# A chunked mLSTM cell and its feed-forward block: attention outputs cross DRAM by feature groups, four tokens side by side, on one queue

## The chip, the cores and the metric

The kernel runs on one core of a Trainium2 chip. TensorE multiplies matrices into PSUM, VectorE, ScalarE and GpSimd work element by element, and SyncE (SP) issues most of the DMA transfers. The metric is the device time in microseconds; lower is better.

## The reference

The inputs are q, k, v and an output gate, each of 4 batches x 8 heads x 768 tokens x 40 features in float32, and two gates per head and token. The first half is a recurrence over tokens with a stabilised running maximum `m`; the second half is a two-layer feed-forward block on the outputs.

```python
for t in range(S):
    m_new = np.maximum(f_gate[:, :, t] + m, i_gate[:, :, t])
    f_stab, i_stab = np.exp(f_gate[:, :, t] + m - m_new), np.exp(i_gate[:, :, t] - m_new)
    C = f_stab * C + i_stab * outer(v_t, k_t)          # per batch and head
    n, m = f_stab * n + i_stab * k_t, m_new
    y[:, :, t] = sigmoid(o_t) * (C @ q_t) / np.maximum(np.abs(n @ q_t), 1.0)
x = y.transpose(0, 2, 1, 3).reshape(B * S, H * D)      # 3072 tokens x 320 features
h = x @ w_in                                           # 320 x 2048
out = (h * sigmoid(1.702 * h)) @ w_out                 # 2048 x 320
```

## The kernel before, in words

**Windows.** The 768 tokens are cut into six windows `w` of 128 tokens. Inside a window the recurrence is written as masked products (`scores`, `values`); from window to window a state is carried (`scale`, `carry`, `decay`). Each window has 4 batches; from w = 1 on, attention works on two pairs of batches, `c` = 0 and 1. The feed-forward block then takes the 4 x 128 = 512 tokens of the window at once: `up_fast` (first layer with GELU, tokens as columns) and `down_fast` (second layer, tokens as rows); for w = 0 these are `up` and `down`.

**Order of work.** Instructions of each engine run in the order in which the program is written; there is no scheduler. While `down_fast(w)` gives TensorE 14 blocks of products (for w = 0 `down` gives 16), the attention of window w + 1 is put between them: `attention` (L786) holds a list of steps and, in `at`, the block after which each stands. For w + 1 > 1 these are: `columns`, the two `scale` and the two `decay` after block 0, `carry` after 3, `scores` after 4, `values` and `seam_in` of c = 0 after 5 and of c = 1 after 6, `seam_turn` of c = 0 after 10 and of c = 1 after 12. For w + 1 = 1 they are spread over 16 blocks, `seam_turn` after 13 and 14.

**Outputs and the turn.** `outputs` (L410) ends with two VectorE instructions (L424), one for each batch of the pair; each writes 128 tokens (partitions) x 320 features of the tile `y`. The feed-forward block needs features on partitions and tokens as columns, `xT`. For w = 0 TensorE transposes (`seam`). For w > 0 `y` goes through a DRAM tile: `x_row<-y` writes both batches in one transfer (L431), and `seam_in` (L489) brings them back in eight loads of 32 rows each, four of 64 and four of 32 features wide (L495), into a free part of `q_sq`, so that `seam_turn` (L497) can finish with VectorE's transposition of 32 x 32 blocks (L499). For c = 0 the write and all loads are on SP's queue; for c = 1 the write and four loads are on ScalarE's, four loads on SP's.

**Stores.** `down_fast` (L705) makes two output tiles `o` per `c` from a pool of two buffers. `product` (L715) adds a PSUM result to a part of `o` on VectorE (L721, L723); `store` (L725) sends one batch's 128 x 320 rows to `out` (L727): store(1) after block 5 or 12, store(0) after 6 or 13. The first products of c = 1 write into the buffers that the stores of c = 0 read. PSUM results come from a pool of four buffers.

**Semaphores of transfers.** Each transfer is given one of eight semaphores in turn, over both queues, and its instruction waits until the transfer that had that semaphore before has landed. A waiting instruction holds up all that stands behind it on its queue.

**GpSimd.** For each window it runs two `scale` (L514, `vw` from v), two `decay` (L507, `state_mid`), then the masks of `weights` (L385). `scale` needs ScalarE's L329, `decay` its L333, which comes after it. `carry` (L516) multiplies `k` with `vw` on TensorE (L524) and adds to `state_mid` on VectorE (L533).

Of the kernel before, what the change touches and what calls it, by code (L numbers as in the profile page):

```python
# [8 lines left out]
FP = mybir.dt.float32  # L9
# [8 lines left out]
L = 128  # L18
# [8 lines left out]
def kernel(  # L27
# [12 lines left out]
    nc = tc.nc  # L40
    B, H, S, D = q.shape
    BH = B * H
    DM = H * D
# [21 lines left out]
    rows = ctx.enter_context(tc.tile_pool(name="rows", bufs=2, space=bass.MemoryType.DRAM))  # L65
# [154 lines left out]
    kT, qT, ys, xT, gs, o_ps, sums, vw, x_row = {}, {}, {}, {}, {}, {}, {}, {}, {}  # L220
# [189 lines left out]
    def outputs(w, hs, u):  # L410

        n = hs.stop - hs.start
        c, b = divmod(hs.start // H, 2)
        den = work.tile([L, n, 1], FP, tag="den", name="den")
        V.tensor_scalar(out=den, in0=u[:, :, D:D1], scalar1=-1.0, scalar2=1.0, op0=OP.mult, op1=OP.max)
        V.tensor_tensor(out=den, in0=u[:, :, D:D1], in1=den, op=OP.max)
        V.reciprocal(out=den, in_=den)
        z = eo[w][:, hs, :]
        V.scalar_tensor_tensor(out=z, in0=z, scalar=1.0, in1=u[:, :, 0:D], op0=OP.add, op1=OP.mult)  # L419
        if b == 0:  # L420
            ys[w, c] = work.tile([L, 2, DM + 64], FP, tag="y", name="y")
        for x in range(n // H):
            y, h = ys[w, c][:, b + x], slice(hs.start + x * H, hs.start + x * H + H)
            V.scalar_tensor_tensor(out=y[:, 0:DM].rearrange("p (h d) -> p h d", d=D), in0=eo[w][:, h, :], scalar=0.5,  # L424
                                   in1=den[:, x * H:(x + 1) * H].to_broadcast([L, H, D]), op0=OP.mult, op1=OP.mult)
        y = ys[w, c][:, b:b + n // H]
        if w == 0:
            G.tensor_copy(out=y[:, :, DM:DM + 64], in_=y[:, :, DM - 64:DM])
            return
        x = x_row[w, c] = rows.tile([2 * L, DM], FP, name="x_row")  # L430
        (nc.scalar if c else nc.sync).dma_start(out=x.rearrange("(b t) d -> t b d", b=2), in_=y[:, :, 0:DM])  # L431

    def values(w, c):
        if w == 0:
            hs = slice(c * H, (c + 1) * H)
            po = ps_m.tile([L, H, D1], FP, tag="m", name="p_o")
            for p in range(NP):
                for i in range(2):
                    h = 2 * p + i
                    T.matmul(po[:, h, :], wt[w, c][:, p, i, :], v_st[:, c * H + h, :], start=True, stop=True)  # L440
            outputs(w, hs, po)
            return
# [21 lines left out]
        V.tensor_tensor(out=v, in0=view(pi), in1=g.to_broadcast([L, 2, NJ, D1]), op=OP.mult)  # L464
        V.tensor_tensor(out=v, in0=view(po), in1=v, op=OP.add)  # L465
        outputs(w, hs, u)

    def x_of(w):
# [15 lines left out]
    def x_square(c, n):  # L484

        at, m = (c * 768, 64) if n == 0 else (c * 768 + 512, 32)
        return q_sq[:, at:at + 8 * m].rearrange("r (b y) -> r b y", y=m)

    def seam_in(w, c):  # L489
        x = x_row[w, c].rearrange("(b r) d -> r b d", r=32)  # L490
        for n, m in ((0, 64), (1, 32)):
            for g in range(4):
                at = g * 64 if n == 0 else 256 + g % 2 * 32
                queue = nc.scalar if c and g % 2 else nc.sync
                queue.dma_start(out=x_square(c, n)[g * 32:g * 32 + 32], in_=x[:, :, at:at + m])  # L495

    def seam_turn(w, c):  # L497
        for n, k in ((0, slice(0, 2)), (1, slice(2, 3))):
# [200 lines left out]
    def last_sums(w, c, js):  # L699

        for j in js:
            s2 = sums[w, 2, j // 2][:, j % 2, :, c]
            V.tensor_tensor(out=s2, in0=hidden(w, j + 4, 0)[:, :, c], in1=s2, op=OP.subtract)

    def down_fast(w, c):  # L705
        o = [op.tile([128, DM], FP, tag="o", name="o_sb") for _ in range(2)]
        o00, o01, o10, o11 = (o[i][:, n * DH:(n + 1) * DH] for i in range(2) for n in range(2))

        def block(two, k):
            return lambda f: gs[w, k * 4 + f // 2][:, f % 2, (2 * c + two) * L:(2 * c + two + 1) * L]  # L710

        def total(x):
            return lambda f: sums[w, x, f // 4][:, f // 2 % 2, f % 2, c, :]

        def product(a, b, *adds):  # L715
            po = ps_m.tile([128, DH], FP, tag="m", name="p_out")
            for f in range(NH):
                T.matmul(po, a(f), b[:, f, :], start=(f == 0), stop=(f == NH - 1))  # L718
            for dst, x in adds:
                if x is None:  # L720
                    V.tensor_copy(out=dst, in_=po)  # L721
                else:
                    V.tensor_tensor(out=dst, in0=x, in1=po, op=OP.add)  # L723

        def store(two):  # L725
            b = 2 * c + two
            nc.sync.dma_start(out=out[b * S + w * L:b * S + (w + 1) * L, :], in_=o[two])  # L727

        return [lambda: product(block(0, 0), w00, (o11, None)),
                lambda: product(block(0, 1), w10, (o00, o11)),  # L730
                lambda: (product(total(2), t2, (o01, o11)), last_sums(w, c, (0, 1))),
                lambda: product(block(1, 0), w01, (o10, o01)),
                lambda: (last_sums(w, c, (2, 3)), product(total(1), t1, (o11, o10), (o01, o01))),
                lambda: (product(block(1, 1), t4, (o10, o10)), store(1)),
                lambda: (product(total(2), w11, (o01, o01)), store(0))]


# [47 lines left out]

    def attention(w):  # L786
        at = (0, 1, 3, 3, 5, 6, 8, 9, 13, 14) if w == 1 else (0, 0, 1, 3, 1, 4, 5, 6, 10, 12)
        calls = [[(columns, w), (scale, w, 0), (scale, w, 1), (decay, w, 0, 0), (decay, w, 1, 0)],
                 [(weights, w, 0)], [(weights, w, 1)], [(carry, w, 0), (carry, w, 1)], [(open_gates, w)],
                 [(scores, w, 0), (scores, w, 1)], [(values, w, 0), (seam_in, w, 0)], [(values, w, 1), (seam_in, w, 1)],  # L790
                 [(seam_turn, w, 0)], [(seam_turn, w, 1)]]
        side = {}
        for i, c in zip(at, calls):
            side.setdefault(i, []).extend(c)
        return side

    for w in range(NW):
# [19 lines left out]
        else:  # L817
# [20 lines left out]
            gelu_fast(w, NF // 2 - 1)  # L838
            run([(hidden_sums, w, j, late) for late in (False, True) for j in (2, 3)])
        side = attention(w + 1) if more else {}  # L840
        if w == 0:
            columns_turn(1)
# [47 lines left out]
```

## Time and profile before

| | |
|---|---|
| time, median of 3 runs | 489.41 us (488.73 to 489.68) |
| time of the profiled execution | 493.03 us |
| its span, first to last instruction | 491.3 us |
| mean granted TensorE clock | 0.997 |
| write `x_row<-y`, issue to landing (median) | 2.3 us on SP, 2.7 us on ScalarE's queue |
| loads `q_sq<-x_row`, 64 KB, issue to landing (median) | 2.2 us on SP, 2.4 us on ScalarE's queue |
| stores `out_dram<-o_sb`, 160 KB, issue to landing (median) | 1.9 us |
| issue of one load `q_sq<-x_row` on SP (median) | 0.45 us |

The profile is of one execution, which took somewhat longer than the runs without a profile. Times in its views count from the first instruction. A wait is put down to the instruction or transfer that ended it last; L-numbers are lines of the kernel before. PE is TensorE, PEld its weight loads, DVE VectorE, ACT ScalarE, POOL GpSimd, and SPq and ACTq are the queues of SyncE and ScalarE. "xT", "x_row", "o_sb" and the like are tiles by the program's names.

### The profile page before, as it was taken

The page shows a single profiled execution, that of the slowest core. Times are in us where ns is not written, and L with a number is a line of the kernel's source. Part 1 is how long each engine was busy: PE and PEld are TensorE (multiplying, and loading weights), DVE is VectorE, ACT ScalarE, POOL GpSimd, SP SyncE. Part 2 cuts the span into 40 slices and gives each one's busy share as a digit, 9 for nine tenths or more (in the row PEclk, how much of TensorE's full clock was granted, in tenths as well). Part 3 has the DMA queues.
Part 4 walks back from the last instruction along what each step waited for, and adds up shares of the span by engine and source line. Part 5 has one row for each costly group of instructions (what it writes and reads, how often), then busy time and mean ns, then how long its engine had stood idle before and what let it go on. Part 6 is the DMA issues. An engine that isn't in the chain of part 4 may idle for free. (4 is left out here: it accounts for less than half of the span.)

```text
span 491.3 us, 12085 instructions
## 1 busy us (share of the span) xinstructions
PE 475.3 (97%) x4926; PEld 380.6 (77%) x4926; DVE 348.1 (71%) x691; ACT 189.8 (39%) x429; POOL 148.8 (30%) x135
## 2 busy tenths in 40 slices
PE   8999999999999999999999999999999999999997
PEld 5774446776678889767889867899877899776997
DVE  5675976987788974868974968984968963653822
ACT  3745559700354800444900254810254810064200
POOL 6020004300397800127610137720136720035300
PEclk9999999999999999999999999999999999899999
DMA  8999987004998214999204899104799304100000
GB/s 182 175 313 142 261 124 197 3 29 119 205 153 121 27 44 104 168 165 131 42 29 121 149 179 141 38 17 128 142 163 136 67 17 111 50 2 0 1 27 29
DMA packets 160472, 52.20 MB, mean 106 GB/s; under 512 B 132736, under 2 KB 157856, under 8 KB 160416
## 3 DMA queue, kind: packets, MB, share of 16 engines
q1 hardware_dynamic: 153616, 48.80, 53.9%
q10 hardware_dynamic: 6800, 2.62, 1.9%
q8 instruction: 39, 0.64, 0.6%
q14 instruction: 17, 0.14, 0.1%
HBM read 43.86 MB, written 7.54 MB: 105 GB/s over the span
## 5 line engine op out<-in xcount | busy, mean ns | idle before, releaser
L658 POOL TENSOR_TENSOR g<-g,parts 128x512 f32<-128x512 f32 x30 | 38.3, 1276 | 221.2 <-DVE parts L650 210.1
L646 ACT COPY parts<-p_h 128x256 f32<-128x256 f32 x40 | 15.0, 374 | 168.1 <-DMA out_dram<-o_sb 84.8
L718 PE MATMUL p_out<-w_out_sb,g 128*128 128x160 f32 x480 | 71.0, 302 | 3.7 <-DVE g L694 3.5
L718 PEld LDWEIGHTS p_out<-w_out_sb,g 128*128 128x128 f32 x480 | 66.8, 190 | 5.9 <-DVE g L694 4.5
L616 PE MATMUL p_h<-xT,w_in_sb 128*128 128x256 f32 x240 | 67.0, 388 | 0.8 <-DVE xT L499 0.8
L597 ACT ACTIVATE g<-g 128x512 f32<-128x512 f32 x80 | 50.0, 631 | 36.0 <-DVE g L653 24.8
L616 PEld LDWEIGHTS p_h<-xT,w_in_sb 128*128 128x128 f32 x240 | 43.6, 190 | 21.3 <-issue 7.6
L723 DVE TENSOR_TENSOR o_sb<-o_sb,p_out 128x160 f32<-128x160 f32 x70 | 20.4, 316 | 48.8 <-DMA out_dram<-o_sb 28.3
L718 PE MATMUL p_out<-t_sb,s 128*128 128x160 f32 x320 | 47.1, 300 | 0.0
L718 PEld LDWEIGHTS p_out<-t_sb,s 128*128 128x128 f32 x320 | 44.4, 190 | 0.2
L649 DVE TENSOR_TENSOR t_x<-p_h,parts 128x256 f32<-128x256 f32 x40 | 16.7, 417 | 39.2 <-PE p_h L621 34.7
L616 PE MATMUL p_h<-t_x,s_in 128*128 128x256 f32 x160 | 41.1, 379 | 0.7 <-DVE t_x L586 0.7
L621 PE MATMUL p_h<-xT,w_in_x 64*128 64x512 f32 x160 | 39.7, 615 | 0.0
L381 ACT ACTIVATE wt<-wt,cols 128x64 f32<-128x64 f32 x160 | 38.8, 335 | 0.1
L667 PE MATMUL p_out<-w_out_sb,g 128*128 128x320 f32 x128 | 36.0, 436 | 0.7 <-DVE w_out_sb L234 0.7
L514 POOL TENSOR_TENSOR vw<-v_st,cols 128x656 f32<-128x656 f32 x12 | 18.9, 1593 | 57.3 <-ACT cols L329 57.3
L616 PEld LDWEIGHTS p_h<-t_x,s_in 128*128 128x128 f32 x160 | 30.3, 190 | 5.2 <-issue 1.1
L667 PEld LDWEIGHTS p_out<-w_out_sb,g 128*128 128x128 f32 x128 | 23.8, 190 | 10.6 <-DVE w_out_sb L234 1.2
L650 DVE TENSOR_TENSOR parts<-p_h,t_x 128x512 f32<-128x512 f32 x40 | 27.7, 692 | 3.5
L546 PE MATMUL p_h<-xT,w_in_sb 128*128 128x512 f32 x64 | 29.5, 604 | 0.1
L657 ACT COPY g<-p_h 128x512 f32<-128x512 f32 x30 | 17.4, 581 | 31.4 <-PE p_h L621 26.1
L653 DVE TENSOR_TENSOR g<-p_h,parts 128x512 f32<-128x512 f32 x40 | 27.7, 691 | 1.4
(185 smaller groups left out, 845.8 us busy)
## 6 DMA issues: line engine op xcount, KB each, us to landing
wt<-m_row SPq DMA_DIRECT2D x40, 128.0 KB, 3.8
k_sq<-in_k_dram SPq DMA_DIRECT2D x16, 320.0 KB, 6.3
q_sq<-in_q_dram SPq DMA_DIRECT2D x16, 320.0 KB, 10.3
out_dram<-o_sb SPq DMA_DIRECT2D x24, 160.0 KB, 1.9
eo<-in_o_gate_dram SPq DMA_DIRECT2D x5, 640.0 KB, 9.5
bits<-in_moe_w_in_dram SPq DMA_DIRECT2D x6, 512.0 KB, 6.9
v_st<-in_v_dram SPq DMA_DIRECT2D x14, 160.0 KB, 4.7
bits<-in_moe_w_out_dram SPq DMA_DIRECT2D x6, 320.0 KB, 5.5
```

What stands on the lines that cost most here:

```text
L381: A.activation(out=x[:, h, :], in_=x[:, h, :], func=AF.Exp, scale=-1.0, bias=cols[w][:, c * PH + h:c * PH + h + 1])
L514: G.tensor_tensor(out=vw[w, c], in0=v_st[:, hs, :], in1=e, op=OP.mult)
L546: T.matmul(ph[j][i], w_in_sb[:, c, f * 128:(f + 1) * 128], x[:, c, :], start=(first and c == 0), stop=(not first and c == 1))
L597: A.activation(out=gs[w, j][:, i, :], in_=gs[w, j][:, i, :], func=AF.Gelu_apprx_sigmoid)
L616: T.matmul(out, a, x[n], start=start, stop=stop)
L621: T.matmul(row, w_in_x[r, j, :], rest_x[r, 2, :], start=not late, stop=late)
L650: V.tensor_tensor(out=y[:, half_w:3 * half_w].rearrange("p (a t) -> p a t", a=2), in0=flat[:, half_w:3 * half_w].rearrange("p (a t) -> p a ...
L653: V.tensor_tensor(out=g[:, 1, :], in0=row1, in1=y[:, half_w:3 * half_w], op=OP.add)
L658: G.tensor_tensor(out=g0, in0=g0, in1=u, op=OP.add)
L667: T.matmul(po, gs[w, f // 2][:, f % 2, b * L:(b + 1) * L], w_out_sb[:, f, :], start=(f == 0), stop=(f == NF - 1))
L718: T.matmul(po, a(f), b[:, f, :], start=(f == 0), stop=(f == NH - 1))
L723: V.tensor_tensor(out=dst, in0=x, in1=po, op=OP.add)
```

## The change

`seam_out` replaces the one write per pair: after each of the two L424 instructions two transfers go out, one for features 0 to 255 as four groups of 64 and one for features 256 to 319 as two groups of 32, into two DRAM tiles laid out by group, then token, then feature. In such a group four consecutive tokens lie side by side, so `seam_in` reads lines of 4 x 64 floats (1 KB) or 4 x 32 floats (512 B): one load of 128 partitions and two of 64 (the 32-wide part is needed on two halves of the partitions). That is four writes and three loads for each `c`, all on SP's queue. Partition r of a block of 32 now holds tokens 4r to 4r + 3 where it held tokens r, 32 + r and so on; the columns of `xT` therefore stand in the order 32 n + r for token 4 r + n, all products keep that order, and `store` of `down_fast` writes rows to DRAM with a step of four: an access of 4 x 32 x 320 in place of 128 x 320. The stores of `down` (w = 0) stay as they are. Apart from this, the list in `attention` puts the two `decay` ahead of the two `scale`.

```diff
--- before.py
+++ after.py
@@ -423,12 +423,11 @@
             y, h = ys[w, c][:, b + x], slice(hs.start + x * H, hs.start + x * H + H)
             V.scalar_tensor_tensor(out=y[:, 0:DM].rearrange("p (h d) -> p h d", d=D), in0=eo[w][:, h, :], scalar=0.5,
                                    in1=den[:, x * H:(x + 1) * H].to_broadcast([L, H, D]), op0=OP.mult, op1=OP.mult)
-        y = ys[w, c][:, b:b + n // H]
-        if w == 0:
+            if w:
+                seam_out(w, c, x)
+        if w == 0:
+            y = ys[w, c][:, b:b + n // H]
             G.tensor_copy(out=y[:, :, DM:DM + 64], in_=y[:, :, DM - 64:DM])
-            return
-        x = x_row[w, c] = rows.tile([2 * L, DM], FP, name="x_row")
-        (nc.scalar if c else nc.sync).dma_start(out=x.rearrange("(b t) d -> t b d", b=2), in_=y[:, :, 0:DM])
 
     def values(w, c):
         if w == 0:
@@ -486,13 +485,23 @@
         at, m = (c * 768, 64) if n == 0 else (c * 768 + 512, 32)
         return q_sq[:, at:at + 8 * m].rearrange("r (b y) -> r b y", y=m)
 
+    def seam_out(w, c, b):
+
+        if b == 0:
+            x_row[w, c] = (rows.tile([2, 4, L, 64], FP, name="x_row"), rows.tile([2, 2, L, 32], FP, name="x_rest"))
+        y = ys[w, c][:, b, :]
+        for x, at, m in ((x_row[w, c][0], 0, 64), (x_row[w, c][1], 256, 32)):
+            g = x.shape[1]
+            nc.sync.dma_start(out=x[b].rearrange("g t y -> t g y"),
+                              in_=y[:, at:at + g * m].rearrange("t (g y) -> t g y", y=m))
+
     def seam_in(w, c):
-        x = x_row[w, c].rearrange("(b r) d -> r b d", r=32)
-        for n, m in ((0, 64), (1, 32)):
-            for g in range(4):
-                at = g * 64 if n == 0 else 256 + g % 2 * 32
-                queue = nc.scalar if c and g % 2 else nc.sync
-                queue.dma_start(out=x_square(c, n)[g * 32:g * 32 + 32], in_=x[:, :, at:at + m])
+        for n, gs_ in ((0, (0,)), (1, (0, 64))):
+            x = x_row[w, c][n]
+            g, y = x.shape[1], x.shape[3]
+            for r in gs_:
+                nc.sync.dma_start(out=x_square(c, n)[r:r + g * 32].rearrange("p (b n) y -> p b (n y)", b=2),
+                                  in_=x.rearrange("b g (r n) y -> (g r) b (n y)", n=4))
 
     def seam_turn(w, c):
         for n, k in ((0, slice(0, 2)), (1, slice(2, 3))):
@@ -724,7 +733,8 @@
 
         def store(two):
             b = 2 * c + two
-            nc.sync.dma_start(out=out[b * S + w * L:b * S + (w + 1) * L, :], in_=o[two])
+            nc.sync.dma_start(out=out[b * S + w * L:b * S + (w + 1) * L, :].rearrange("(r n) d -> n r d", n=4),
+                              in_=o[two])
 
         return [lambda: product(block(0, 0), w00, (o11, None)),
                 lambda: product(block(0, 1), w10, (o00, o11)),
@@ -785,7 +795,7 @@
 
     def attention(w):
         at = (0, 1, 3, 3, 5, 6, 8, 9, 13, 14) if w == 1 else (0, 0, 1, 3, 1, 4, 5, 6, 10, 12)
-        calls = [[(columns, w), (scale, w, 0), (scale, w, 1), (decay, w, 0, 0), (decay, w, 1, 0)],
+        calls = [[(columns, w), (decay, w, 0, 0), (decay, w, 1, 0), (scale, w, 0), (scale, w, 1)],
                  [(weights, w, 0)], [(weights, w, 1)], [(carry, w, 0), (carry, w, 1)], [(open_gates, w)],
                  [(scores, w, 0), (scores, w, 1)], [(values, w, 0), (seam_in, w, 0)], [(values, w, 1), (seam_in, w, 1)],
                  [(seam_turn, w, 0)], [(seam_turn, w, 1)]]
```

## The prediction

> **What bounds the kernel now.** I read the page's busy shares first:
>
> ```profile
> PE 475.3 (97%) x4926; PEld 380.6 (77%) x4926; DVE 348.1 (71%) x691; ACT 189.8 (39%) x429; POOL 148.8 (30%) x135
> ```
>
> TensorE sets the time, so the edit is worth only the TensorE gaps that it opens or closes. Next, the waits of all engines; columns: total us, times, longest.
>
> ```profile
> DVE o_sb L723 <- DMA out_dram<-o_sb: 28.3, 4, 8.2
> ...
> PE p_out L718 <- DVE o_sb L723: 2.5, 3, 1.9
> ...
> PE p_h L616 <- DVE xT L499: 0.8, 1, 0.8
> PE p_h L616 <- DVE t_x L586: 0.7, 1, 0.7
> ```
>
> VectorE stands four times, about 7 us each, until an output store has landed (L723 overwrites a store buffer), and TensorE runs out of PSUM buffers behind it: the timeline puts these gaps at 194.08 (0.35), 269.23 (0.25) and 418.84 (1.88). The last two lines are at 121.79 and 124.15, where stage w=1 waits for its transposed tokens. Why is the store late? SP's own waits, then the chain around 410 us (start, us, what):
>
> ```profile
> SPq L727 <- DMA q_sq<-x_row: 13.1, 4, 3.8
> ```
>
> ```profile
> 410.04 2.88 DMA x_row<-y
> 412.92 0.02 issue
> 412.94 3.52 DMA q_sq<-x_row
> ...
> 416.52 1.82 DMA out_dram<-o_sb
> ...
> 418.47 0.33 DVE o_sb L723
> 418.80 0.04 issue
> 418.84 6.29 PE p_out L718 x32
> ```
>
> The program gives each transfer one of eight semaphores in turn, and a transfer waits until that semaphore's former holder has landed. The built program shows store(0) of c=0 taking the one of the first load that ScalarE issues for c=1. So a store whose data is there at 405.9 waits for c=1's write (410.04 to 412.92) and first load (to 416.46). Last, stretches around the 1.88 us gap; columns: us, busy PE, PEld, DVE, ACT, POOL, granted clock, DMA share, GB/s.
>
> ```profile
> 416.90:418.80 1.90, 0.06 (x1) 0.00 (x0) 0.33 (x2) 0.00 (x0) 0.00 (x0) 1.00 0.55 149
> ...
> 419.90:423.30 3.40, 3.40 (x15) 3.40 (x14) 2.85 (x9) 0.00 (x0) 0.00 (x0) 0.50 0.02 2
> ```
>
> After the gap TensorE runs 3.4 us at half clock: the 32 matmul records at 418.84 take 6.29, the like 32 at 182.60 take 4.61. That is 1.68 us more, not counted as idle anywhere.
>
> **What the Trainium skill says.** "TensorE: Matmul & The Clock Gate", What's actually happening: the clock falls to one half after an idle window and returns after a busy one of about 3.4 us. The trace agrees on the half and the 3.4 us, but 1.9 us of idling was enough here. "DMA: Bandwidth & Descriptors", Why a DMA increments its semaphore by 16 and not by 1: a transfer runs on the largest number of engines, up to 16, that divides the slowest dimension of both sides. The new store's DRAM side is 4 x 32 rows, so 4 engines; every transfer before has 16 or a multiple outermost, and no run here shows the other. Same page, Issuing engines are not separate DMA queues: a second issuing engine saves only issue time. In the trace ScalarE's four loads take 3.20 us to issue beside SP's, waits included. Same page, Specifications: lines under 512 B miss full rate. The new writes have 256 and 128 B; the one row like them, the 128 B lines of st_row at 59.5 us, landed in 3.7 us behind other loads.
>
> **The change part by part.** Sums are against the profiled execution's 491.3 us span (493.03 as timed); its median unprofiled is 489.41. I carry the difference over unscaled.
>
> *The way through DRAM.* Last stage: the two y halves of c=0 (L424, 0.45 each) end at 405.2 and 405.64. Before: one write at 405.66 landing in 3.1 (2.3 in other stages), eight loads issued 408.82 to 412.70, store(0) at 416.52, landed 418.35. After: the first half's writes go out at 405.25. Issue is about 0.6 for 512 lines (the 512-line wt loads: 0.63) and 0.45 for 256 (the old loads), so four take 2.1 and the second pair starts at 406.3. Landing I take between 2.3 (the old write) and 3.7 (st_row). Then x_row's second half is in at 408.6 to 410.0 and x_rest's at 409.3 to 410.7; three loads of 0.45, and store(0) is at the head of SP at 410.2 to 411.6. It now waits for a semaphore whose holder, store(1), landed long ago. With its own 3.2 (below) it lands at 413.4 to 414.8, 3.6 to 5 us earlier. TensorE's four PSUM buffers last to 416.9. The gap goes: 1.88, and with it the half clock: 1.68. By the same shift the gaps 0.35 and 0.25 go. Late next is block 12's copy, paced by TensorE itself.
>
> Queued behind on SP: c=1's four writes (data at 409.55, free queue at 410.6 to 412.0) and three loads, the last landing at 417.3 to 420.0 against about 420.4 before. seam_turn of c=1 stands after block 12, about 419; a late one delays only token_sums after block 13. The ScalarE queue loses five DMA issues a stage; it sat idle 30 us there, so that is worth nothing.
>
> *Stage w=0 to w=1*, where TensorE does wait for tokens. Before: VectorE idles 2.62 until 120.63 for a store, then L499 four times to 123.19, then L586 at 123.59. After, everything is 298.0 earlier than the figures above: store b0 is out by 113.6 on 16 engines (w=0 stores are not reordered), so L671 and c=0's transposes run at 118.0, and c=1's last load lands at 119.3 to 122.0. The first gap (0.76) goes. The second needs x1 by 121.04 + 1.62 (three products) = 122.66; from landing there are 1.07 of transposes, 0.45 copy and 0.42 L586, so it goes wholly for a landing by 120.7, else some 0.6 stays. Gain 0.9 to 1.5, taken 1.3.
>
> *The stores.* Twenty stores spread over 4 engines. In the last store's own packets:
>
> ```profile
> 489.40:490.10 0.70, 0.00 (x0) 0.00 (x0) 0.00 (x0) 0.00 (x0) 0.00 (x0) 1.00 0.66 234
> ```
>
> 0.70 x 0.66 x 16 / 128 rows is 58 ns a row. Eight rows an engine are 0.46, 32 are 1.85: +1.39. All but the last store are hidden (by 2 us and more, as shown for store(0); without that cover each would cost up to 1.39). The last, issued at 488.58 and landing in 1.8, ends the kernel: +1.39. Bounds: 0, if it still spreads over 16, and 2.0 if rows on few engines or the store before it (issued 2.2 earlier) hold it up. No gain is possible there.
>
> *GpSimd's order.* Stage w=2:
>
> ```profile
> 161.21 3.34 POOL L514 TENSOR_TENSOR vw<-v_st,cols 128x656 f32<-128x656 f32 x2 [3.12 <-ACT cols L329]
> 164.52 1.88 POOL L507 TENSOR_TENSOR state_mid<-state,cols 128x328 f32<-128x328 f32 x2
> ```
>
> Decays need ScalarE's L333, which ends at 161.56, so GpSimd starts 0.4 later: decays to 163.5, scalings to 165.15 and 166.82. TensorE's carry (L524) starts at 165.90 and wants the second scaling half of 2.08 later, 166.94. It is there with 0.1 to spare; the last stage gives 391.56 against 391.72, w=1 85.3 against 86.0. No gain either, as L533 comes at 168.10, after the old decays too. GpSimd's L385 starts 0.4 later, and a 0.45 wait for ScalarE absorbs it. Cost 0, at most 0.3 in each of four stages, 1.2.
>
> Sum: -1.3 -0.60 -1.88 -1.68 +1.39 = -4.07: span 487.2, median 489.41 - 4.1 = 485.3 us.
>
> **Rivals.** *Stores keep 16 engines*: no tail, 484.0. For it: nothing in the trace; against: the page's rule.
>
> *Mostly hidden*: the half clock hangs on where windows fall and need not be in the unprofiled median (-1.68 lost), w=1 gains 0.9, GpSimd costs 0.8: -0.9 -0.6 -1.88 +1.39 +0.8 = -1.2, 488.2; with tail 2.0 it is 488.8, no change. For it: the gap falls into one of three like stages only.
>
> *Slower: short lines into DRAM through one queue.* If the 256 and 128 B writes land in over 7.5 us, store(0) lands at Y + 12.7, Y the end of the second y half, where it lands now; that is the turning point. At 9 us the gap of 1.5 us more comes in four stages (+6.0), c=1's loads follow by twice that and hold w=1's start for some 3, and the tail adds 1.4: 499. Against: st_row's 3.7 us, with other loads ahead of it; the DMA engines are near idle here.
>
> **How the numbers follow.** No change is within 0.2%, about what a measurement of this kernel can tell: 488.4 to 490.4. Forecast 0.64, 16 engines 0.12, mostly hidden 0.14 (half of it within 0.2%), slower 0.10. So faster 0.82, same 0.08, slower 0.10. The range runs from the 16-engine case with w=1's full gain (483.7) to the upper edge of the hidden case: 483.5 to 488.8.
>
> **What would show it.** Right: no VectorE wait over 3 us for the store at L723, no TensorE gap before block 12 in the last stage, clock 1.00 through it, landings of reordered stores near 3.2 and the span's end 1.4 further from the last VectorE instruction. Wrong: gaps at L524 for POOL; x_row landing beyond 5 us; store(0) still behind loads.

## The result, and the profile after

The changed kernel takes 488.23 us (median of 20 runs, 487.28 to 490.68); beside it the kernel before took 490.26 (20 runs, 488.73 to 492.37). The ratio is 0.996, with a 95% interval of 0.9948 to 0.9972. So it is faster, by 2.0 us, just under half of the 4.1 forecast.

The profiled execution after took 487.78 us, with a span of 486.1 us and a mean granted clock of 0.998; its one half-clock stretch begins at 484.0, when TensorE has ended. That of before had 493.03 and 491.3: by the two profiles the gain is 5.2 us, by the medians 2.0. That discrepancy is the first thing to explain.

The busy shares of the page after:

```profile
PE 471.6 (97%) x4926; PEld 378.4 (78%) x4926; DVE 348.3 (72%) x691; ACT 189.7 (39%) x429; POOL 149.3 (31%) x135
```

TensorE still sets the time, and its busy time fell by 3.7 us with the same 4926 matmuls. Fewer gaps don't lower busy time; a clock that stays up does: the half-clock stretch of before was worth 1.7 us, and a second profile of before, below, which has no such stretch while TensorE works, has 472.3 us busy where the first has 475.3. The rest of the fall is spread over the span and was not traced.

The largest of TensorE's waits in the first profile of before (total us, times, longest):

```profile
PE p_out L718 <- DVE g L694: 3.5, 4, 0.9
```

TensorE's waits after:

```profile
PE p_c L533 <- POOL vw L523: 3.5, 8, 0.6
...
PE p_h L625 <- DVE t_x L595: 0.9, 1, 0.9
```

The 2.5 us for L723 (now L732) are gone, and so are the 3.5 us for VectorE's L694 (now L703). In their place stand eight waits, two in each of four stages, for GpSimd's scalings, and a slightly longer one for t_x. The waits of all engines after have this line for the stores:

```profile
DVE o_sb L732 <- DMA out_dram<-o_sb: 20.3, 4, 5.8
```

VectorE still waits for each store, 5 us instead of 7, and that is now short enough for TensorE's PSUM buffers. SyncE's queue in the last stage (start, us, what):

```profile
405.88 0.36 SPq L503 DMA_DIRECT2D q_sq<-x_row  x1
406.34 1.26 SPq L503 DMA_DIRECT2D q_sq<-x_rest  x2
407.69 0.59 SPq L736 DMA_DIRECT2D out_dram<-o_sb  x1
...
413.98 0.36 SPq L503 DMA_DIRECT2D q_sq<-x_row  x1
414.45 1.25 SPq L503 DMA_DIRECT2D q_sq<-x_rest  x2
```

The store follows the three loads at once (407.69; before it was 416.52). Two neighbouring lines of the chain that ended last show what this gives TensorE:

```profile
402.31 15.41 PE p_out L727 x112
417.72 3.06 PE p_h L625 x14
```

The stretch that had the 1.88 us gap and 6.29 us of slow matmuls is now one unbroken block. Last, the end of the span, after VectorE's last instruction (480.86 to 481.18); columns: us, busy PE, PEld, DVE, ACT, POOL, granted clock, DMA share, GB/s:

```profile
481.20:481.90 0.70, 0.00 (x0) 0.00 (x0) 0.00 (x0) 0.00 (x0) 0.00 (x0) 1.00 0.26 95
481.90:484.00 2.10, 0.00 (x0) 0.00 (x0) 0.00 (x0) 0.00 (x0) 0.00 (x0) 0.99 0.26 77
```

A share of 0.26 is about 4 of 16 DMA engines. Before, the last store's packets were 0.70 us at a share of 0.66.

### The profile page after: what moved, and what is told of

It reads as the page before. It is cut to its first block, busy times and chain, and to the rows that moved or that the text cites. A ratio compares the mean times of both kernels' runs of the same rounds, so it can differ in the third digit from the quotient of the medians.

```text
span 486.1 us, 12090 instructions
## 1 busy us (share of the span) xinstructions
PE 471.6 (97%) x4926; PEld 378.4 (78%) x4926; DVE 348.3 (72%) x691; ACT 189.7 (39%) x429; POOL 149.3 (31%) x135
## 4 chain that ended last, share of the span: by engine, by line
PE 62%; POOL 10%; SPq 8%; DVE 6%; DMA 6%; issue 5%; ACT 2%; DVEq 0%; POOLq 0%
PE p_out L727 25%; PE p_h L625 15%; PE p_h L630 5%; PE p_h L555 4%; DMA wt<-m_row 3%; SPq L363 3%; PE p_o L449 2%; POOL vw L523 2%; SPq L119 2%; PE p_i L457 2%; POOL g L667 2%; SPq L311 2%; PE p_s L405 2%; PE p_out L676 1%; PE p_c L533 1%
## 5 line engine op out<-in xcount | busy, mean ns | idle before, releaser
L727 PE MATMUL p_out<-w_out_sb,g 128*128 128x160 f32 x480 | 69.6, 301 | 0.1
L732 DVE TENSOR_TENSOR o_sb<-o_sb,p_out 128x160 f32<-128x160 f32 x70 | 20.5, 315 | 41.5 <-PE p_out L727 20.8
L516 POOL TENSOR_TENSOR state_mid<-state,cols 128x328 f32<-128x328 f32 x10 | 11.4, 1155 | 59.4 <-ACT cols L333 55.6
```

## Experiments

Each kernel is given by its difference from the changed kernel or from the kernel before, and was timed in five rounds together with the kernel before. Experiments 1 to 4 ran on one chip, 5, 7, 8 and 9 on another and 6 on a third. Where two profiles are compared instruction by instruction, "shift" is how much later TensorE starts the same matmul.

**1. The kernel before, once more.** No edit.

> The kernel before, unchanged, profiled again. Theory 1 (the profiled execution of before was not typical: its last stage held a TensorE gap of 1.88 us and then 3.4 us at half clock, worth some 3.1 us over its sister stages): this profile has a gap below 0.7 us ahead of block 12 of the last stage, no half-clock stretch there, and a span of 488 to 489.3 us. Theory 2 (that gap and the half clock are in every execution, as the prediction's sum has it): gap 1.7 to 2.0, half clock for 3.4 us after it, span 490.5 to 491.5. Time against before: the same within 0.2% in both.

Measured: 490.17 us (22 runs) against 490.46 (51 runs), ratio 0.9987 (0.9974 to 1.0001): two sets of runs of one program differ by 0.1%. Its profile has a span of 488.1 us and clock 1.00. TensorE's wait in it and the stretches round it:

```profile
PE p_out L718 <- DVE o_sb L723: 2.6, 2, 2.1
```

```profile
415.40:417.20 1.80, 0.00 (x0) 0.00 (x0) 0.30 (x2) 0.00 (x0) 0.00 (x0) 1.00 0.48 140
417.30:419.90 2.60, 2.60 (x19) 2.60 (x20) 2.60 (x9) 0.00 (x0) 0.00 (x0) 1.00 0.20 32
419.90:423.30 3.40, 3.40 (x23) 3.22 (x22) 3.02 (x11) 0.37 (x1) 0.00 (x0) 1.00 0.18 63
```

The gap in the last stage is there again, up to 417.28 and 2.07 us long, even longer than in the first profile. The half clock after it is not: 1.00 where the first profile had 0.50. The gap is in both profiles of the kernel, the half clock in one. Only 6 of the 51 runs had a mean clock of 0.997 or less, as the first profile had, and they took 491.1 to 493.3 us. "TensorE: Matmul & The Clock Gate", What's actually happening, in the Trainium skill, lets the clock fall after an idle window of about 3.4 us; here a shorter one of 1.88 us was followed by half clock and one of 2.07 us was not, so the length of the gap alone does not decide. The profiles of the other experiments agree: 3.4 us at half clock came after idle times of 1.32 (experiment 3), 1.50 (7) and 2.04 us (9), and none after 1.53 (5) and 1.56 us (3).

This second profile, 0.4 us below its kernel's median as the profile after is, is the fair partner for after: spans 488.1 and 486.1, a difference of 2.0, that of the medians. Most of the accounting below uses it.

**2 and 3. GpSimd's order apart.** In experiment 2 the changed kernel gets the old order back; in 3 the kernel before gets the new order alone.

```diff
 # 2, on the changed kernel
-[(columns, w), (decay, w, 0, 0), (decay, w, 1, 0), (scale, w, 0), (scale, w, 1)]
+[(columns, w), (scale, w, 0), (scale, w, 1), (decay, w, 0, 0), (decay, w, 1, 0)]
 # 3, on the kernel before
-[(columns, w), (scale, w, 0), (scale, w, 1), (decay, w, 0, 0), (decay, w, 1, 0)]
+[(columns, w), (decay, w, 0, 0), (decay, w, 1, 0), (scale, w, 0), (scale, w, 1)]
```

> The changed kernel with GpSimd's scalings ahead of its decays again, as before. Theory 1 (read from the two traces: the new order removes four TensorE waits of 0.9 us for VectorE's L694 and brings waits of 1.0 us in all for the scalings, and shortens what follows by 0.3): about 1.3 us slower than the changed kernel, the waits for the scalings gone, the four waits for L694 back. Prediction's reading (the order is worth nothing): within 0.3 us of the changed kernel.

> The kernel before with GpSimd's decays ahead of its scalings and nothing else. Theory 1: 1.0 to 1.6 us faster than before. Prediction's reading: 0 to 1.2 us slower.

Measured: 2 takes 489.43 us (21 runs), ratio 0.998 (0.9969 to 0.9991), so about 0.2% of the change's 0.4% is gone; 3 takes 490.13 (13 runs), ratio 0.9992 (0.9972 to 1.0012), not told from no change. The waits show the same switch in both. In the profile of 2:

```profile
PE p_out L727 <- DVE g L703: 3.5, 4, 0.9
```

In that of 3:

```profile
PE p_c L524 <- POOL vw L514: 3.4, 8, 0.6
```

Either TensorE waits four times for VectorE's L694, or eight times for GpSimd. VectorE at w = 2 in the first profile of before (start, us, what; GpSimd's rows stand in the prediction):

```profile
161.63 3.47 DVE L694 TENSOR_TENSOR g<-g 128x512 f32<-128x512 f32 x2
```

and GpSimd, then VectorE, in after:

```profile
160.90 2.42 POOL L516 TENSOR_TENSOR state_mid<-state,cols 128x328 f32<-128x328 f32 x2 [3.56 <-ACT cols L333]
163.29 2.71 POOL L523 TENSOR_TENSOR vw<-v_st,cols 128x656 f32<-128x656 f32 x2
```

```profile
160.91 1.82 DVE L703 TENSOR_TENSOR g<-g 128x512 f32<-128x512 f32 x2
```

VectorE's L694 (L703 in after) is the same subtraction in both. With GpSimd's scalings beside them, two take 3.47 us, 1.77 each; with the decays, 1.82, the first 0.68 and the second 1.22; in the last stage, where GpSimd runs nothing beside them, each takes 0.68 in either kernel. Both engines' instructions stretch: the two decays take 2.42 us there and 1.88 in before, where they come when L694 is nearly done. "SBUF — State Buffer", Who interferes with whom, in the Trainium skill says that a VectorE instruction with two SBUF inputs contends with a GpSimd instruction that reads SBUF; L694 and the scalings are such a pair, and so are L694 and the decays. The rows agree that they hold each other up, and the single instructions show that they take turns. In after, L703's first ends at 161.59, the decay beside it 0.60 later, L703's second 0.54 after that and the second decay 0.60 after that; in before, L694's first ends 0.55 after the first scaling, the second scaling 1.14 after that and L694's second 0.55 after that. So VectorE waits out the long scalings in the one order and the short decays in the other.

The shifts of after against experiment 1's profile give the price in a stage: about -1.15 where the wait for L694 went, +0.65 and +0.5 at the two carries that now wait for the scalings, and -0.35 to -0.4 at the next scores in three of the four stages. So the exchange of waits is even (0.88 us for L694 against 0.58 and 0.28 at the carries), and what is gained is gained at the scores, whose 128 matmuls take 2.46 us in before and 2.10 in after at w = 2; what they waited for was not traced. In all it is about -1.4 over four stages. Experiment 3's profile has the same four terms, but stood 0.9 behind by the stage to w = 1 and ran at half clock after a wait near 257, so its span says nothing on the order. Such stretches weigh on its median too: 5 of its 13 runs have a mean clock of 0.997 or less, against the 6 of 51. What the order is worth in the medians lies between the 0.3 us of experiment 3 and the 1.0 by which 2 stands behind after; the intervals allow both, and it stays open to that extent.

**4. Stores on all engines again.** The changed kernel with the old form of the store.

```diff
-nc.sync.dma_start(out=out[...].rearrange("(r n) d -> n r d", n=4), in_=o[two])
+nc.sync.dma_start(out=out[...], in_=o[two])
```

> The changed kernel with each store writing 128 contiguous rows again, so that it can spread over 16 engines; what is left out is putting the token rows back in their order, so the rows of a window stand permuted in the output. Theory 1: the last store lands in about 1.8 us and the time from the last VectorE instruction to the span's end falls from 4.9 to about 2.7 us; the whole is 2.0 to 2.3 us faster than the changed kernel. Prediction's size: 1.4 us faster. Rival (stores on few engines also hold up VectorE between the halves): over 3 us faster.

Measured: 486.37 us (485.71 to 487.04, 4 runs), ratio 0.9914 (0.9891 to 0.9936), so 4.1 us below the kernel before where after is 2.0 below. (It leaves out putting the rows back in order, so it is a measure and not a replacement.) Its last store's packets, in its profile:

```profile
482.50:483.30 0.80, 0.00 (x0) 0.00 (x0) 0.00 (x0) 0.00 (x0) 0.00 (x0) 1.00 0.61 215
483.30:484.10 0.80, 0.00 (x0) 0.00 (x0) 0.00 (x0) 0.00 (x0) 0.00 (x0) 1.00 0.00 0
```

They are through in 0.8 us. From VectorE's last instruction to the end of the span it takes 484.8 - 481.68 = 3.1 us, against 486.1 - 481.18 = 4.9 in after; VectorE itself ends 0.5 later than in after. So the form of the store costs some 2 us, all at the very end. The order of tokens that the new loads bring is paid for there.

**5. A third order.** GpSimd: first decay, both scalings, second decay.

```diff
-[(columns, w), (decay, w, 0, 0), (decay, w, 1, 0), (scale, w, 0), (scale, w, 1)]
+[(columns, w), (decay, w, 0, 0), (scale, w, 0), (scale, w, 1), (decay, w, 1, 0)]
```

> The changed kernel with GpSimd's order decay 0, scaling 0, scaling 1, decay 1. If the two waits of each stage are what the order does (scalings first stretch VectorE's L694, 3.47 us for two beside them against 1.82 beside the decays; decays first make the first product of carry wait for its scaling), this order should have neither: no TensorE wait for GpSimd at carry, none or under 0.3 us for VectorE's subtraction ahead of it, and 3 to 4 us less than the changed kernel. If VectorE is stretched by any GpSimd work just there, the waits for it stay at 0.5 to 0.9 a stage and nothing or under 1.5 us is gained.

Measured: 489.03 us (9 runs), the kernel before 490.87 (30 runs), ratio 0.9967 (0.9945 to 0.9988): no better than after's 0.996. Yet the waits did shrink:

```profile
PE p_c L533 <- POOL vw L523: 1.0, 4, 0.3
```

No wait for L703 came back. Against after, each stage gains 0.7 at the carries; 0.4 is lost again at p_o in the stages to w = 2, 3 and 4, and TensorE ends 0.45 later than in after. GpSimd and VectorE at w = 2, in after and, second, in this kernel, show where the first loss comes from:

```profile
165.96 4.14 POOL L385 TENSOR_SCALAR_AFFINE_SELECT wt<-wt 64x1024 f32<-64x1024 f32 x3
167.03 0.60 DVE L516 TENSOR_TENSOR state<-state_mid,cols 128x328 f32<-128x328 f32 x1
```

```profile
166.44 3.96 POOL L385 TENSOR_SCALAR_AFFINE_SELECT wt<-wt 64x1024 f32<-64x1024 f32 x3
166.63 1.29 DVE L516 TENSOR_TENSOR state<-state_mid,cols 128x328 f32<-128x328 f32 x1
```

The second decay, now last, puts off GpSimd's masks (L385), so that the first of them has just begun when VectorE comes to its own decay, L516. In both kernels that L516 ends some 0.35 after the first mask does (167.29 in after, 167.58 here); in after it waits little, here it waits out nearly the whole mask and takes 1.29 instead of 0.60. So VectorE loses the 0.7 it had gained and reaches the product of scores and masks no earlier in the stage than in after. That TensorE's p_o waits for this product is read from the program, not tested. The contention was moved, not removed. The rest of what was lost, at waits before p_i of up to 1.5 that the profile puts down to nothing, was not traced further.

**6. The last store in four.** The changed kernel, with its last store alone cut into four of 32 rows.

```diff
+rows_out = out[...].rearrange("(r n) d -> n r d", n=4)
+if w == NW - 1 and b == 2:
+    for n in range(4):
+        (nc.scalar if n % 2 else nc.sync).dma_start(out=rows_out[n], in_=o[two][n * 32:n * 32 + 32, :])
+    return
```

> The changed kernel with its very last store cut into four transfers of 32 rows each, two issued by SyncE and two by ScalarE. Theory (the last store is slow because its outermost dimension of 4 puts 128 rows on 4 DMA engines, 32 rows of some 67 ns each): each transfer of 32 rows can use 16 engines, its rows take a fraction of the 2.2 us, and a second issue of about 0.4 us comes after the first; the distance from VectorE's last instruction to the end of the span falls from 4.9 us to about 3.9, and the time by about 1.0 us, to some 487.3 where the kernel before has 490.4: ratio 0.993 to 0.995. Rival (the tail is the store's fixed cost or the rows' step of four in DRAM, not the number of engines): distance stays at 4.9 or grows by the second issue, time as the changed kernel, ratio 0.996 to 0.997.

Measured: 487.4 us (486.76 to 488.03, 6 runs), the kernel before 490.23 (11 runs), ratio 0.994 (0.9919 to 0.9962). Its end:

```profile
481.30:482.00 0.70, 0.00 (x0) 0.00 (x0) 0.00 (x0) 0.00 (x0) 0.00 (x0) 1.00 0.27 97
482.00:483.00 1.00, 0.00 (x0) 0.00 (x0) 0.00 (x0) 0.00 (x0) 0.00 (x0) 1.00 0.73 200
483.00:484.00 1.00, 0.00 (x0) 0.00 (x0) 0.00 (x0) 0.00 (x0) 0.00 (x0) 0.91 0.09 21
```

The share rises to 0.73, the last packets are through at about 483.6, 2.3 after VectorE's last instruction (in after at about 484.7, 3.5 after it), and from VectorE's last instruction to the end it is 485.4 - 481.3 = 4.1 us. The rows still go to DRAM with a step of four, so the number of engines and not the step made the store slow. What comes after the packets is longer than in after (1.8 against 1.4); the runs don't show why. By its median this version is ahead of both kernels: 2.8 us below the kernel before, against 2.0. The intervals of the two ratios overlap; the shorter end is what the profiles show.

**7. Five and six together.** Both edits.

> The changed kernel with that mixed order and, for the very last store alone, four stores of 32 rows, two on SP's and two on ScalarE's queue, in place of one that runs on four DMA engines. The end after the last VectorE instruction should fall from 4.9 us to about 3.2 (0.4 above before's 2.75 for the second issue on each queue). With the mixed order's gain of 3 to 4 us: 4.5 to 6 us less than the changed kernel, about 483 us.

Measured: 487.14 us (6 runs), ratio 0.9942 (0.9922 to 0.9961): the same as experiment 6. By the medians the third order adds nothing here either. In its profile 3.4 us at half clock follow the idle time of 1.50 us at w = 3, and two of the six runs, at 488.62 and 489.07 us, have a mean clock of 0.995 or less, where the other four have a median of 486.7; whether the order is worth something at full clock, so few runs don't tell.

**8. The second pair on ScalarE's queue.** The changed kernel, with the writes and loads of c = 1 issued by ScalarE.

```diff
-            nc.sync.dma_start(out=x[b].rearrange("g t y -> t g y"), ...
+            (nc.scalar if c else nc.sync).dma_start(out=x[b].rearrange("g t y -> t g y"), ...
-                nc.sync.dma_start(out=x_square(c, n)[r:r + g * 32]...
+                (nc.scalar if c else nc.sync).dma_start(out=x_square(c, n)[r:r + g * 32]...
```

> The changed kernel with the four writes and three loads of c = 1 on ScalarE's queue instead of SP's. If the one queue is what keeps the stage w=0 to w=1 from gaining (c=1's first write goes out at 113.73, 2.2 us after its data, because SP is busy with c=0's), c=1's tokens land 1.5 to 2 us earlier, the TensorE wait of 0.9 us for L595 goes, and the time falls by 0.6 to 1.0 us. If landing and not the queue is what takes long, nothing changes beyond 0.3 us.

Measured: 495.63 us (494.51 to 498.18, 6 runs), ratio 1.0112 (1.0091 to 1.0132), the slowest of all. TensorE's waits:

```profile
PE p_h L625 <- DVE t_x L595: 3.2, 1, 3.2
PE p_h L625 <- DVE xT L508: 2.5, 1, 2.5
```

Both are in the stage to w = 1. ScalarE's queue there:

```profile
116.07 0.37 ACTq L503 DMA_DIRECT2D q_sq<-x_row  x1
120.62 1.31 ACTq L503 DMA_DIRECT2D q_sq<-x_rest  x2
```

SyncE's queue in this kernel and, second, in after:

```profile
114.07 3.26 SPq L107 DMA_DIRECT2D k_sq<-in_k_dram  x4
```

```profile
118.23 0.36 SPq L503 DMA_DIRECT2D q_sq<-x_row  x1
118.75 1.24 SPq L503 DMA_DIRECT2D q_sq<-x_rest  x2
120.09 0.53 SPq L681 DMA_DIRECT2D out_dram<-o_sb  x1
120.66 2.10 SPq L107 DMA_DIRECT2D k_sq<-in_k_dram  x4
```

With c = 1 off SyncE's queue, nothing holds back the next window's k: four transfers of 320 KB go out 6.6 us earlier, ahead of the three loads of c = 1 (256, 64 and 64 KB) that TensorE needs next. The stretches of this kernel and, second, of after show the DMA share (the last figure but one):

```profile
116.00:118.00 2.00, 2.00 (x9) 1.45 (x8) 1.97 (x5) 0.00 (x0) 0.00 (x0) 1.00 1.02 225
```

```profile
116.00:118.00 2.00, 2.00 (x9) 1.43 (x8) 1.97 (x5) 0.00 (x0) 0.00 (x0) 1.00 0.35 66
```

The x_rest loads then took 5.9 us to land, and 6.8 us at half clock followed, from 124.6. One queue is thus not only a place to stand in line: its order is what keeps bulk transfers behind urgent ones. Which wait held the x_rest loads on ScalarE's queue from 116.4 to 120.6 is not shown.

**9. One queue alone.** The kernel before with its eight loads of 32 rows, all x_row transfers on SyncE's queue.

```diff
-(nc.scalar if c else nc.sync).dma_start(out=x.rearrange("(b t) d -> t b d", b=2), in_=y[:, :, 0:DM])
+nc.sync.dma_start(out=x.rearrange("(b t) d -> t b d", b=2), in_=y[:, :, 0:DM])
-                queue = nc.scalar if c and g % 2 else nc.sync
+                queue = nc.sync
```

> The kernel before with all its writes and loads of x_row on SP's queue, and nothing else: the store(0) of c = 0 no longer shares a semaphore with a load of c = 1. If that shared semaphore is what made the store late (as the prediction says), store(0) goes out right behind c = 0's eight loads, some 3 us earlier, VectorE's waits for it fall below 5 us and the TensorE gaps ahead of block 12 go: 2.5 to 3.3 us, less 0 to 1.3 us for later tokens of c = 1 at w=1, so 1.2 to 3.3 us less than before. If the fewer and longer loads are what frees the store, the gaps stay and the time is that of before or above.

Measured: 491.7 us (22 runs), ratio 1.0014 (0.9997 to 1.0032). TensorE's waits:

```profile
PE p_h L616 <- DVE t_x L586: 3.1, 2, 2.0
...
PE p_out L718 <- DVE o_sb L723: 0.2, 1, 0.2
```

SyncE's queue in the last stage:

```profile
409.63 3.78 SPq L495 DMA_DIRECT2D q_sq<-x_row  x8
413.51 0.39 SPq L727 DMA_DIRECT2D out_dram<-o_sb  x1
414.00 0.38 SPq L431 DMA_DIRECT2D x_row<-y  x1
418.38 3.77 SPq L495 DMA_DIRECT2D q_sq<-x_row  x8
```

The store is issued as soon as the eight loads are, with no wait for another queue's transfer (in experiment 1's profile it stood 4.5 us more behind the same eight), and the gap at block 12 is gone: shifts of -0.7 and -1.8 against experiment 1's profile, in the stages to w = 2 and in the last. But c = 1's eight loads now take 3.77 us of issue where after's three take 1.6, and its tokens come late: +1.4 in the stage to w = 1, +1.2 in the last. The wait of 2.04 us in the stage to w = 1 is followed by 3.4 us at half clock, which add 1.6; and this is not the profile's alone: 15 of the 22 runs have a mean clock of 0.997 or less, against 7 of the 30 of the kernel before. The other seven have a median of 489.65, where the other 23 of before have 490.53. So the single queue by itself removes the store gaps, and late tokens and the half clock after them take as much again. That the fewer, longer loads make it pay follows from after, which has no wait over 0.9 us there; no run has them alone.

## Where the prediction was wrong, and where right

All sums in us; the third column is the shift from before's first profile, the fourth from experiment 1's.

| step | forecast | first profile to after | experiment 1 to after |
|---|---|---|---|
| stage w = 0 to w = 1 | -1.3 | -0.7 | +0.5 |
| gaps at the stores | -0.60 -1.88 | -3.5 | -3.4 |
| half clock | -1.68 | -1.7 | 0 |
| GpSimd's order | 0 | -1.3 | -1.4 |
| last store | +1.39 | +2.2 | +2.1 |
| sum | -4.07 | -5.0 | -2.2 |
| span, measured | | -5.2 | -2.0 |

The residues of 0.2 are small shifts at the start and between stages.

**Gaps at the stores: right, by its mechanism.** The store did wait for a semaphore held by a load on the other queue (experiment 9), and did go out behind c = 0's three loads. On the forecast's clock it was due 4.95 to 6.35 after the first writes; they went out at 401.67 and it at 407.69, 6.0 later. It then took up to 4.4 to land (VectorE, which waits for it, goes on at 412.09), not the 3.2 taken, and that was still in time. One sign named for being right did not come: VectorE's waits for the store at L723 stayed over 3 us, 5.1 in the mean (7.1 before). Against experiment 1 the four stages gain 0.8, 0.2, 0.1 and 2.3, where the forecast had 0.35, 0.25, nothing and 1.88: the mechanism held, and the gaps differ from execution to execution.

**Half clock: the step that failed first.** "The gap goes: 1.88, and with it the half clock: 1.68" was true of the profiled execution and was then carried "over unscaled" to the median. Experiment 1 shows the same gap without it, and only 6 of 51 runs have the low clock that goes with it. The profile of before gave a warning: its execution took 493.03 us, above all three runs shown (at most 489.68), and half clock was a thing that could make it so. The "mostly hidden" rival named exactly this loss, gave 488.2 us, and got a chance of 0.14; the measured time is that number by luck: its gain was 1.2 us from a base of 489.41, the measured one 2.0 from 490.26, by other terms than the rival's.

**Stage w = 0 to w = 1: failed; not -1.3, and against experiment 1 a loss.** The two gaps of 0.76 and 0.74 were taken as typical. In experiment 1 VectorE's wait for the store there is 1.20, not 2.62; the first gap is absent and the second is 0.62. There was 0.6 to win, not 1.5 (1.0 in experiment 3's profile, which has the old loads too). And it wasn't won: TensorE's waits there are 0.9 in after. The last load of c = 1 was forecast to land between 119.3 and 122.0, with a full gain only by 120.7. After's VectorE rows:

```profile
121.06 0.71 DVE L508 STREAM_TRANSPOSE xT<-q_sq 128x512 f32<-128x512 f32 x1 [1.72 <-DMA q_sq<-x_row]
121.95 0.45 DVE L508 STREAM_TRANSPOSE xT<-q_sq 128x256 f32<-128x256 f32 x1 [0.17 <-DMA q_sq<-x_rest]
...
122.86 0.41 DVE L595 TENSOR_TENSOR t_x<-xT 128x256 f32<-128x256 f32 x1
```

It landed at 121.95, the late edge: c = 1's loads stand in one queue behind c = 0's and a store, and then wait 2.4 for their own write to land. In experiment 1 VectorE's L586 starts at 122.26; its counterpart here, L595, at 122.86. The range for the landing was right, and the step took its better end.

**GpSimd's order: failed; not 0 but -1.4 in the profiles, 0.3 to 1.0 by the medians.** Two things were missed. The row with the wait on L694 (3.5 us, the largest of TensorE's waits before) was on the page, and the step never asked why a 512-wide subtraction should take 1.77 us where its neighbours take 0.69; the answer stood in the same stage, GpSimd's scalings. And "there with 0.1 to spare" at the second half of the scalings took TensorE's arrival at the carry, 165.90, as given, though it came after that very wait. GpSimd's four instructions ended 5.1 us after the first began, as forecast (5.2); but TensorE arrives about 1.15 earlier and now waits for both scalings. These are the gaps at L524 for POOL that the prediction named as a sign of being wrong. They take back what the lost wait gave, and the gain that is left comes at the scores, which the step did not look at.

**Last store: right in kind, mis-sized.** Four engines, as "DMA: Bandwidth & Descriptors", Why a DMA increments its semaphore by 16 and not by 1, in the Trainium skill had it, and as the share of 0.26 shows. The term was 24 further rows at 58 ns; it measured 67 to 69 ns a row on four engines, 32 of which take 2.2 us, and its issue takes 0.54 to 0.59 instead of 0.33 to 0.36. Its packets also start at 482.40, 1.2 after VectorE's last instruction (0.9 in experiment 1), as those of the store before it end. From VectorE's last instruction to the end it was 2.8 in experiment 1 and is 4.9: +2.1, just above the bound of 2.0 given for it.

**The rivals.** That the stores keep 16 engines fell (0.26). Short lines did no such harm: the x_row writes (256 B lines) landed in 2.4 us by the page's median, and the x_rest transfers, writes of 128 B lines among them, in 3.6 at most, far from the turning point of 7.5.

From the forecast to the measured: half clock 1.68, w = 1 1.8 and the last store 0.7 were too hopeful, together 4.2; GpSimd 1.4 and the store gaps 0.9 too cautious, together 2.3; 1.9 remain, and with 0.2 of residue that is the 2.1 by which the gain fell short. The rest of the distance from 485.3 to 488.23, 0.9, is that of the base: 490.26 in these runs against 489.41 in the three shown.

## What to carry to other kernels

Before a stall's aftermath is put into a sum, compare the profiled execution's own time with the unprofiled runs: where it lies above them all, what is seen once in it, a half clock or a gap in one of several like stages, is a suspect and not a term. When a transfer's rows are reordered, ask how many DMA engines its outermost dimension leaves, and cut the one that ends the kernel. And when a queue is freed, look at what else it lets through: its order may be all that keeps bulk loads behind urgent ones.

## What was not expected of the hardware

- TensorE's idle times of 1.32, 1.50, 1.88 and 2.04 us were followed by 3.4 us at half clock, others of 1.53, 1.56 and 2.07 us by none.
- A 128 x 512 subtraction on VectorE takes 0.68 us with nothing beside it, 1.77 beside GpSimd's 128 x 656 products and 0.68 or 1.22 beside its 128 x 328 ones: the instructions of the two engines end in turn. VectorE's own 128 x 328 product takes 1.29 us instead of 0.60 where a mask instruction of GpSimd has just begun.
- Rows of 1280 B on four DMA engines took 67 to 69 ns each, against 58 in the store that had all sixteen.
